# Attention scores in four hand-turned PSUM banks, and weight and operand work spread over the head pairs of a fused attention and two-layer feed-forward kernel

## The chip, the cores and the metric

One core of a Trainium2 chip runs the whole program in one launch. The metric is the device time of one execution in microseconds; the median over the runs is compared. Engines: TensorE (PE, its weight loads PEld), VectorE (DVE), ScalarE (ACT), GpSimd (POOL), and SyncE (SP), whose queue issues nearly all DMAs.

## The reference

```python
batch, n_heads, seq, head_dim = (4, 8, 576, 64)
def _attn_ref(q, k, v, f):
    scores = scale * np.matmul(q, k.transpose(0, 1, 3, 2))
    cum = np.cumsum(np.log(np.clip(f, 0.0001, 1.0)), axis=-1)
    decay = cum[:, :, :, None] - cum[:, :, None, :]
    scores = np.where(causal, -1000000000.0, scores + decay)
    scores = scores - np.max(scores, axis=-1, keepdims=True)
    attn = np.exp(scores)
    attn = attn / (np.sum(attn, axis=-1, keepdims=True) + 1e-09)
    return np.matmul(attn, v)
# x = attention as 2304 rows of 512, then two layers, d_ff = 2048:
# h = x @ w_in;  g = h * clip(h + 3, 0, 6) / 6;                    x = g @ w_out
# h = x @ w_in2; g = max(h, 0) + alpha * min(h, 0);              out = g @ w_out2
```

## The kernel before

There are 16 head pairs (4 batches of 4 pairs, two heads of 64 columns each). The attention runs over 144 units, nine to a pair: positions 0 to 3 are four blocks of 128 query rows of the even head, position 4 is the tail (the last 64 query rows of both heads together, against all 576 keys, in two halves of 288 columns), positions 5 to 8 are the odd head's four blocks. A loop over steps `t` runs a software pipeline in a fixed order on every engine: at step `t` PE transposes the probabilities of unit `t-5`, DVE takes the negated row maximum of unit `t-1` (`maxes`), ACT takes the exponentials with row sums of unit `t-2` (`exps`), ACT or DVE copies the transposed probabilities out of PSUM (`evac`), then the work due at this step (`todo`) and the score matmuls of unit `t` (`stage1`) are issued, and last what a table puts beside the step (`aside`). Nothing is reordered later: each engine works its list from the front.

The scores of a unit go to one of four PSUM banks in turn (`ps_sc`); the tail takes two. A bank is written again four or three units later, once the exponential that reads it is done.

Due work by its position in a pair: at 3 and 7, POOL scales and copies the next head's q and k (`prep_head`, tiles q1, k1); two steps later POOL forms the low part of k (`low_k`); `low_q`, on DVE, forms the low part of q (tile q2) for the even head at position 6 and the odd head at position 0. `recips` (position 2, of the pair before) inverts the row sums on DVE and widens them on POOL (tile rw), `spread` (5) transposes rw on PE and copies it to rcb, `stage3` (6 and 8) multiplies the transposed probabilities with v into one PSUM bank (pv), and DVE writes pv times rcb into r, the layer input.

Beside the units runs preparation for the first layer. A weight step converts 128x512 packed 64-bit weights to f32: m on ACT, then f, s, j, g on DVE; sums S1 to S4 on POOL, casts h on ACT, low parts l on POOL. `build_parts` makes seven sums of blocks of r: a (in place, POOL), h (cast, ACT), l (low part, POOL), each for two columns. The tables `CONV_ATT` and `CONV_ATT1` and the list `places` give the step of each; a name such as `j1 34` is step j of weight chunk 1 at step 34.

After the attention, PE works without a break through the two layers (lines 633 on), 24 sets of products and pieces in each; the last attention steps (`DRAIN`) already issue the first products.

Of the kernel before, what the change touches and what calls it, by code (L numbers as in the profile page):

```python
# [8 lines left out]
F32 = mybir.dt.float32  # L9
# [4 lines left out]
AF = mybir.ActivationFunctionType  # L14
# [7 lines left out]
def decay_attention_ffn2_kernel(ctx, tc, qk, v, f, wi1, wo1, wi2, wo2, alpha, out):  # L22
# [22 lines left out]
    DRAIN = {9 * NP + 3: 2, 9 * NP + 4: 2, 9 * NP + 6: 2, 9 * NP + 7: 2}  # L45
    CONV_ATT = "m0 22 f0 23 s0 24 j0 25 g0 26 m1 31 f1 32 s1 33 j1 34 g1 35 hb 37 lb 39 S1 42 S3 42 S2 45 S4 45 ha 51 la 54 hc 53 lc 60 hd 60 ld 63 m2 69 f2 70 s2 71 j2 72 g2 73 m3 78 f3 79 s3 80 j3 81 g3 83 ho0 78 lo0 87 ho1 87 lo1 91 wi0 90 wi1 93 wo0 99 wo1 102 r0 54 r1 63 r2 93 r3 104"
    CONV_ATT1 = "r0 131 r1 141 m0 108 f0 109 s0 110 j0 114 g0 115 m1 117 f1 118 s1 119 j1 123 g1 124 S1 143 S3 145 S2 146 ha 146 hc 146 hb 147 la 147 lc 147 lb 148 S4 149 hd 149 ld 150 m2 150 f2 151 s2 151 j2 152 g2 153 m3 151 f3 152 s3 153"
    CONV_FIRST = "j3 0 g3 1 ho0 2 lo0 4 ho1 5 lo1 7 wi0 30 wi1 33 wo0 36 wo1 38"
    CONV_A = "m0 0 f0 2 s0 3 j0 4 g0 5 m1 4 f1 6 s1 7 j1 8 g1 9"
# [69 lines left out]

    def conv_ops(ff, g, cache=False, held=()):  # L120

        ops, stage = {}, {}

        def f32(s):

            if s not in stage:
                tag = {0: "wa", 1: "wb", 2: "wc", 3: "wb", "S": "wc"}[s]
                if cache:
                    tag = ("wa", "wb", "wc")[(4 * g + s) % 3]
                stage[s] = wtmp.tile([128, KH, 256], F32, tag=tag, name=tag)  # L130
            return stage[s]
# [146 lines left out]
    def attention():  # L278
        with ExitStack() as ax:
            rx = ExitStack()  # L280
            rawp = rx.enter_context(tc.tile_pool(name="rawp", bufs=3, side="right"))
            opsp = rx.enter_context(tc.tile_pool(name="opsp", bufs=3, side="right"))
            ps_sc = rx.enter_context(tc.tile_pool(name="ps_sc", bufs=4, space=PSUM, side="right"))
            vp = ax.enter_context(tc.tile_pool(name="vp", bufs=2))
# [54 lines left out]

            def maxes(parts, dsts):  # L340
                n = len(parts)
                nm = st.tile([128, 2], F32, tag="nm", name="nm")
# [4 lines left out]
                return parts, dsts, nm  # L347

            def exps(parts, dsts, nm):
                pt = pp.tile([128, S], F32, tag="p", name="p")  # L350
                for i, (src, c0, cw) in enumerate(parts):
                    nc.scalar.activation(out=pt[:, c0:c0 + cw], in_=src, func=AF.Exp, bias=nm[:, 0:1],  # L352
                                         scale=1.0, accum_out=dsts[i])
                return (pt,)

            def stage1(u):
                p, ab, i = u
                if p not in sm:
                    sm[p] = sums.tile([128, 10], F32, tag="sm", name="sm")
                ss = sm[p]  # L360
                if ab < 2:
                    q1, q2, k1, k2 = slots[2 * p + ab]
                    w = 128 * (i + 1)
                    n = max(w, 256)
                    sc = ps_sc.tile([128, 512], F32, tag="sc", name="sc")
                    qs = slice(128 * i, 128 * i + 128)
                    nc.tensor.matmul(out=sc[:, 0:n], lhsT=q1[:, qs], rhs=k1[:, 0:n], start=True, stop=False)  # L367
                    nc.tensor.matmul(out=sc[:, 0:n], lhsT=q2[:, qs], rhs=k2[:, 0:n], start=False, stop=False)  # L368
                    nc.tensor.matmul(out=sc[:, w - 128:w], lhsT=identb, rhs=maskb, start=False, stop=True)  # L369
                    c = 5 * ab + i  # L370
                    return [(sc[:, 0:w], 0, w)], [ss[:, c:c + 1]]
                parts = []
                hw = S // 2
                for c in range(2):
                    sc = ps_sc.tile([128, 512], F32, tag="sc", name="sc")
                    ks = slice(hw * c, hw * c + hw)
                    for a in range(2):
                        q1, q2, k1, k2 = slots[2 * p + a]
                        nc.tensor.matmul(out=sc[:, 0:hw], lhsT=q1[:, 512:640], rhs=k1[:, ks],
                                         start=(a == 0), stop=False)  # L380
                        nc.tensor.matmul(out=sc[:, 0:hw], lhsT=q2[:, 512:640], rhs=k2[:, ks],
                                         start=False, stop=(a == 1 and c == 0))
                    if c == 1:
                        nc.tensor.matmul(out=sc[:, hw - TAIL:hw], lhsT=identb, rhs=maskj, start=False, stop=True)
                    parts.append((sc[:, 0:hw], hw * c, hw))
                return parts, [ss[:, 4:5], ss[:, 9:10]]

# [31 lines left out]
            def recips(p):  # L419

                ss = sm.pop(p)
                rc = st.tile([128, 10], F32, tag="rc", name="rc")
# [5 lines left out]
                rw = rcp.tile([128, KT, 2, 64], F32, tag="rw", name="rw")  # L428
                scaled(
                    "P", rw, rc.rearrange("p (a i) -> p i a", a=2).unsqueeze(3).broadcast_to([128, KT, 2, 64]))  # L430
                rcs[p] = rw

            def spread(p):

                rw = rcs.pop(p)
# [132 lines left out]
            aside(18, lambda: fetch(1))  # L568
            ops = conv_ops(0, 0, held=(0, 1, 2, 3))
            for name, t in table(CONV_ATT):  # L570
                aside(t, ops[name])
            early["first"] = conv_ops(0, 1, held=(0, 1))
# [4 lines left out]
            for k, (a, h) in enumerate(zip(("", "l0", "l1", "l2", "a3", "a4", "a6", "l3", "l4", "a5", "l6", "l5"),  # L577
                                           ("0", "1", "2", "", "", "", "3", "4", "6", "", "5", ""))):
                for c in range(KH):
                    if a:  # L580
                        aside(places[k], {"l": lows, "a": adds}[a[0]][int(a[1]), c])
                    if h:
                        aside(places[k], highs[int(h), c])
            for t in range(len(units) + max(LV, PB) + 1):
# [13 lines left out]
                if t < len(units):  # L598
# [333 lines left out]
```

## Time and profile before

| | us |
|---|---|
| median of 3 runs | 977.1 (976.98 to 977.2) |
| the profiled execution | 978.46 |
| its span, first to last instruction | 975.4 |
| PE, DVE, ACT, POOL busy in the span | 959.3, 698.8, 539.3, 594.4 |
| granted TensorE clock | 1.0 throughout |

So 3.06 us of the profiled execution lie outside its span, and it took 1.36 us more than the median. A busy matmul is a pipelined one whose end is modelled: rows of PE overlap, and its share of busy time says little. A stretch from one pair's tail to the next pair's tail, cut at the start of the tail's masking matmul (L384), is the unit in which the attention is read below; there are 15 such stretches, and the first has no `stage3` in it.

### The profile page before, as it was taken

To read this page: it belongs to the slowest core of one execution; us is meant where nothing else is said; L and a number is where in the kernel's file an instruction comes from. 1 tells how busy PE (TensorE), PEld (TensorE's weight loads), DVE (VectorE), ACT (ScalarE), POOL (GpSimd) and SP (SyncE) were. 2 spreads that over 40 slices of the span, in tenths; PEclk is the share of its full clock that TensorE was granted. 3 is DMA by queue.
4 is the path that set the end of the run, shared out by engine and by line. 5 is a ranking of instruction groups with operands and counts; after the bars stand their busy time and mean duration, and the time that the engine had idled before them with its cause. 6 is when DMAs were issued, how large, how long until landed. Compare 5 with 4: busy or idle time off the path is not lost.

```text
span 975.4 us, 15895 instructions
## 1 busy us (share of the span) xinstructions
PE 959.3 (98%) x5524; PEld 858.9 (88%) x5525; DVE 698.8 (72%) x1275; ACT 539.3 (55%) x1348; POOL 594.4 (61%) x583
## 2 busy tenths in 40 slices
PE   8999999999999999999999999999999999999998
PEld 5767666678999999999999999989899989989897
DVE  7998878857688777876788665357898778635454
ACT  5778787866555554555564356644455546343231
POOL 7577589957655666487576289556646658422231
PEclk9999999999999999999999999999999999999999
DMA  6656586401424444210578722413524410253541
GB/s 214 217 146 213 158 273 203 151 1 44 162 90 182 184 166 161 107 66 1 173 281 301 289 91 107 162 65 143 196 95 182 184 66 23 97 205 141 215 162 65
DMA packets 36195, 145.79 MB, mean 149 GB/s; under 512 B 4860, under 2 KB 4860, under 8 KB 33012
## 3 DMA queue, kind: packets, MB, share of 16 engines
q1 hardware_dynamic: 36112, 144.79, 42.2%
q8 instruction: 43, 0.70, 0.3%
q14 instruction: 36, 0.29, 0.1%
q10 hardware_dynamic: 4, 0.00, 0.0%
HBM read 97.21 MB, written 43.42 MB: 144 GB/s over the span
## 4 chain that ended last, share of the span: by engine, by line
PE 85%; DVE 7%; POOL 3%; ACT 2%; issue 2%; DMA 1%; SPq 0%; POOLq 0%; DVEq 0%; ACTq 0%
PE o L762 21%; PE hA L722 20%; PE o L760 19%; PE hC L722 10%; PE hB L722 5%; PE pv L457 4%; PE tp L400 2%; DVE nm L344 2%; PE sc L367 2%; PE sc L368 1%; DVE q L336 1%; ACT p L352 1%; POOL xl L248 1%; DVE r L240 1%; DVE pt L411 0%
## 5 line engine op out<-in xcount | busy, mean ns | idle before, releaser
L705 POOL TENSOR_TENSOR g<-t,g 128x384 fp32r<-128x384 f32 x192 | 205.3, 1070 | 285.6 <-ACT g L704 269.1
L760 PE MATMUL o<-g,wo 128*128 128x384 f32 x1152 | 231.0, 339 | 2.1 <-POOL g L705 1.2
L722 PE MATMUL hA<-xh,wi 128*128 128x384 f32 x768 | 224.3, 338 | 0.7 <-ACT s L727 0.4
L762 PE MATMUL o<-wo,g 128*128 128x512 f32 x864 | 223.2, 394 | 0.0
L760 PEld LDWEIGHTS o<-g,wo 128*128 128x128 f32 x1152 | 203.9, 188 | 3.6 <-POOL g L705 1.8
L704 ACT CAST g<-t 128x384 fp32r<-128x384 f32 x192 | 98.7, 514 | 177.5 <-DVE t L699 92.6
L762 PEld LDWEIGHTS o<-wo,g 128*128 128x128 f32 x864 | 160.6, 188 | 25.7
L780 DVE TENSOR_TENSOR r<-o,r 128x512 f32<-128x512 f32 x126 | 86.6, 688 | 86.3 <-PE o L762 85.9
L722 PEld LDWEIGHTS hA<-xh,wi 128*128 128x128 f32 x768 | 141.5, 188 | 4.4 <-ACT s L727 0.7
L722 PE MATMUL hA<-xl,wi 128*128 128x384 f32 x384 | 129.6, 337 | 0.0
L769 DVE SCALAR_TENSOR_TENSOR r<-o,r 128x384 f32<-128x384 f32 x168 | 91.9, 552 | 45.8 <-PE o L760 45.0
L722 PE MATMUL hC<-xh,wi 128*128 128x384 f32 x384 | 114.1, 338 | 0.0
L352 ACT ACTIVATE p<-sc,nm 128x128 f32<-128x128 f32 (+4 forms) x160 | 84.1, 529 | 20.7 <-DVE nm L344 17.3
L344 DVE TENSOR_REDUCE nm<-sc 128x1 f32<-128x128 f32 (+4 forms) x160 | 71.4, 469 | 6.2 <-PE sc L369 4.0
L722 PEld LDWEIGHTS hA<-xl,wi 128*128 128x128 f32 x384 | 72.1, 188 | 3.2
L722 PEld LDWEIGHTS hC<-xh,wi 128*128 128x128 f32 x384 | 70.9, 188 | 2.1 <-issue 0.2
L248 POOL TENSOR_TENSOR xl<-r,xh 128x384 fp32r<-128x384 f32 x59 | 68.9, 1185 | 2.0 <-ACT xh L243 1.5
L400 PE MATMUL tp<-ident,p 128*128 128x128 f32 x384 | 67.6, 279 | 1.1 <-ACT pt L416 0.6
L727 ACT COPY s<-hA 128x384 f32<-128x384 f32 x96 | 45.8, 477 | 34.7 <-PE hA L722 34.4
L722 PE MATMUL hC<-xl,wi 128*128 128x384 f32 x192 | 64.8, 337 | 0.0
L367 PE MATMUL sc<-k,q 128*128 128x256 f32 (+2 forms) x128 | 53.7, 420 | 4.7 <-ACT p L352 3.6
L722 PE MATMUL hB<-xh,wi 128*128 128x384 f32 x192 | 57.1, 338 | 0.0
(136 smaller groups left out, 1724.6 us busy)
## 6 DMA issues: line engine op xcount, KB each, us to landing
wid<-wi SPq DMA_DIRECT2D x24, 896.0 KB
wi<-wid SPq DMA_DIRECT2D x12, 1792.0 KB
rqk<-in_qk SPq DMA_DIRECT2D x32, 608.0 KB
raw<-in_wi SPq DMA_DIRECT2D x32, 512.0 KB
raw<-in_wo SPq DMA_DIRECT2D x32, 512.0 KB
wod<-wo SPq DMA_DIRECT2D x24, 512.0 KB
wo<-wod SPq DMA_DIRECT2D x12, 1024.0 KB
vt<-in_v SPq DMA_DIRECT2D x16, 320.0 KB
```

The source lines that it names most:

```text
L248: e.tensor_sub(out=XS[k][1][:, b, c], in0=x, in1=XS[k][0][:, b, c].bitcast(F32))
L344: nc.vector.tensor_reduce(out=nm[:, i:i + 1], in_=src, axis=AX.X, op=ALU.max, negate=True)
L352: nc.scalar.activation(out=pt[:, c0:c0 + cw], in_=src, func=AF.Exp, bias=nm[:, 0:1], scale=1.0, accum_out=dsts[i])
L367: nc.tensor.matmul(out=sc[:, 0:n], lhsT=q1[:, qs], rhs=k1[:, 0:n], start=True, stop=False)
L400: nc.tensor.transpose(tp[:, j, :], pt[:, 128 * j:128 * j + 128], ident)
L704: nc.scalar.copy(out=gt[n][i][:, 0], in_=hold["g"])
L705: nc.gpsimd.tensor_sub(out=gt[n][i][:, 1], in0=hold["g"], in1=gt[n][i][:, 0].bitcast(F32))
L722: nc.tensor.matmul(out=h, lhsT=a, rhs=b[:, x, kc], start=new and kc + e == 0, stop=kc == KH - 1 and e == 2, skip_group_check=not new)
L760: nc.tensor.matmul(out=o[:, 0:NB], lhsT=a[:, cs], rhs=b, start=st, stop=sp)
L762: nc.tensor.matmul(out=o, lhsT=b[:, cs], rhs=a, start=st, stop=sp)
L769: later(0, lambda: nc.vector.scalar_tensor_tensor(out=acc, in0=o[:, 0:NB], scalar=1.0 / 6.0, in1=acc, op0=ALU.mult, op1=ALU.add))
L780: nc.vector.tensor_add(out=acc, in0=o, in1=acc)
```

## The change

The four score banks become one tile with waits written by hand (the same waits between PE, DVE and ACT as before). The tail's two halves lie in neighbouring banks and are read by one maximum and one exponential over 576 columns, so the minimum of two maxima, the addition of two row sums and a copy go; the row sums need 9 columns in place of 10, rw 512 in place of 640, and the tail's reciprocal goes to PE straight from rc. `low_q` of the even head is issued in front of `stage3` at its step. The tables are new: f and s of a weight chunk now share one step, j and g one step a pair later; the casts h stand about a pair ahead of, or behind, what they go with; the seven sums are spread from the third pair on; one more weight chunk (m2 of `CONV_ATT1`) is moved into the attention. The staging tiles of a weight set get a fourth buffer, wd.

```diff
-    CONV_FIRST = "j3 0 g3 1 ho0 2 lo0 4 ho1 5 lo1 7 wi0 30 wi1 33 wo0 36 wo1 38"
+    BUILD_ATT = "h00 26 l00 32 h01 35 l01 41 h10 44 l10 50 h11 53 l11 79 a30 79 h20 80 a31 88 h21 89 l20 95 a40 97 l21 97 h30 98 l30 104 a41 106 h31 107 h40 107 l31 113 l40 115 a60 115 h41 116 l41 122 a61 124 a50 124 h60 125 a51 130 l60 131 h61 134 h50 134 h51 134 l61 139 l50 140 l51 142"
+    CONV_FIRST = "ho0 0 lo0 2 ho1 4 lo1 6 wi0 30 wi1 33 wo0 36 wo1 38"
...
-                tag = {0: "wa", 1: "wb", 2: "wc", 3: "wb", "S": "wc"}[s]
+                tag = "w" + tags[(0, 1, 2, 3, "S").index(s)]
...
-            ps_sc = rx.enter_context(tc.tile_pool(name="ps_sc", bufs=4, space=PSUM, side="right"))
+            ps_sc = rx.enter_context(tc.tile_pool(name="ps_sc", bufs=1, space=PSUM, side="right"))
+            banks = ps_sc.tile([128, 4, 512], F32, name="sc")
...
-                for i, (src, c0, cw) in enumerate(parts):
-                    nc.vector.tensor_reduce(out=nm[:, i:i + 1], in_=src, axis=AX.X, op=ALU.max, negate=True)
-                if n == 2:
-                    nc.vector.tensor_scalar(out=nm[:, 0:1], in0=nm[:, 0:1], scalar1=nm[:, 1:2], scalar2=None, op0=ALU.min)
+                src = banks[:, b, 0:w] if n == 1 else banks[:, b:b + n, 0:w]
+                last = waits("V", nc.vector.tensor_reduce(out=nm, in_=src, axis=AX.X if n == 1 else AX.XY, op=ALU.max,
+                                                     negate=True), last)
...
-                for i, (src, c0, cw) in enumerate(parts):
-                    nc.scalar.activation(out=pt[:, c0:c0 + cw], in_=src, func=AF.Exp, bias=nm[:, 0:1],
-                                         scale=1.0, accum_out=dsts[i])
+                o = pt[:, 0:src.shape[-1]] if n == 1 else pt.rearrange("p (n w) -> p n w", n=n)
+                last = waits("A", nc.scalar.activation(out=o, in_=src, func=AF.Exp, bias=nm, scale=1.0, accum_out=dst), last)
+                for x in range(b, b + n):
+                    reader[x] = last
...
-                nc.vector.tensor_scalar(out=ss[:, 4:5], in0=ss[:, 4:5], scalar1=ss[:, 9:10], scalar2=None,
-                                        op0=ALU.add)
-                nc.vector.tensor_copy(out=ss[:, 9:10], in_=ss[:, 4:5])
...
-                nc.tensor.transpose(tj[:, 0, :], rw[:, 4].rearrange("p a b -> p (a b)"), ident)
+                nc.tensor.transpose(tj[:, 0, :], rc[:, 8:9].broadcast_to([128, 128]), ident)
...
-            places = [9 * p + o for p in range(9, NP) for o in (5, 9)][1:]
...
+            for name, t in table(BUILD_ATT):
+                aside(t, {"h": highs, "l": lows, "a": adds}[name[0]][int(name[1]), int(name[2])])
...
-                        todo.setdefault(t + QL + 1, []).append(lambda h=2 * p + 2: low_q(h))
+                        todo.setdefault(t + QL + 1, []).insert(0, lambda h=2 * p + 2: low_q(h))
```

DVE from the 13th to the 14th reciprocal, before: nm is the negated maximum, q the low part of q, pt the transposed probabilities, wb a weight chunk.

```order
L427 RECIPROCAL rc<-rc 128x10
L145 TENSOR_SCALAR wb<-wb 128x512
L344 TENSOR_REDUCE nm<-sc 128x1 x2
L411 COPY pt<-tp 128x4x128
L344 TENSOR_REDUCE nm<-sc 128x1 x2
L346 TENSOR_SCALAR nm<-nm 128x1
L344 TENSOR_REDUCE nm<-sc 128x1
L464 TENSOR_TENSOR r_82<-pv,rcb 128x256
L336 SCALAR_TENSOR_TENSOR q_2921<-rqk,q_2920 64x640
L149 SCALAR_TENSOR_TENSOR wb<-raw,wb 128x512
L344 TENSOR_REDUCE nm<-sc 128x1
L154 SCALAR_TENSOR_TENSOR wb<-raw,wb 128x512
```

The same stretch of DVE now; the rest of the pair follows in the order of before, less the addition and the copy of row sums.

```order
L443 RECIPROCAL rc<-rc 128x9
L364 TENSOR_REDUCE nm<-sc 128x1 x2
L430 COPY pt<-tp 128x4x128
L364 TENSOR_REDUCE nm<-sc 128x1 x2
L357 SCALAR_TENSOR_TENSOR q_2729<-rqk,q_2728 64x640
L480 TENSOR_TENSOR r_82<-pv,rcb 128x256
L364 TENSOR_REDUCE nm<-sc 128x1
L150 SCALAR_TENSOR_TENSOR wc<-raw,wc 128x512
L155 SCALAR_TENSOR_TENSOR wc<-raw,wc 128x512
```

One maximum and the minimum are gone, q stands in front of r, and j and g of a chunk stand together with no s before them.

POOL over the pair before that, from one rw to the next: xl and r_80 are low parts and sums of the layer input, k the copies and low parts of k. Before:

```order
L93 TENSOR_SCALAR rw<-rc 128x640
L93 TENSOR_SCALAR q_2711<-rqk 128x640
L93 TENSOR_SCALAR k_2713<-rqk 128x576
L331 TENSOR_TENSOR k_2713<-rqk,k_2713 64x576
L240 TENSOR_TENSOR r_80<-r_80 128x384 x2
L93 TENSOR_SCALAR q_2805<-rqk 128x640
L93 TENSOR_SCALAR k_2807<-rqk 128x576
L331 TENSOR_TENSOR k_2807<-rqk,k_2807 64x576
L240 TENSOR_TENSOR r_80<-r_80 128x384 x2
```

And now:

```order
L94 TENSOR_SCALAR rw<-rc 128x512
L94 TENSOR_SCALAR q_2539<-rqk 128x640
L94 TENSOR_SCALAR k_2541<-rqk 128x576
L352 TENSOR_TENSOR k_2541<-rqk,k_2541 64x576
L249 TENSOR_TENSOR xl_79<-r_80,xh_78 128x384
L94 TENSOR_SCALAR q_2624<-rqk 128x640
L94 TENSOR_SCALAR k_2626<-rqk 128x576
L249 TENSOR_TENSOR xl_79<-r_80,xh_78 128x384
L241 TENSOR_TENSOR r_80<-r_80 128x384
L352 TENSOR_TENSOR k_2626<-rqk,k_2626 64x576
```

Four block instructions beside the pair's own have become three.

## Rows read from the trace of the kernel before

**Rows 1.** Stretches from tail to tail: busy time by engine, clock, DMA share, GB/s.

```profile
core 0: us, PE busy (x) PEld busy (x) DVE busy (x) ACT busy (x) POOL busy (x), PEclk, DMA share, GB/s
24.10:84.95 60.85, 59.55 (x458) 42.47 (x456) 54.34 (x118) 47.06 (x173) 41.28 (x44) 1.00 0.61 190
84.95:195.95 111.00, 106.56 (x822) 76.15 (x820) 92.89 (x213) 87.63 (x319) 90.83 (x87) 1.00 0.63 195
84.95:96.39 11.44, 11.44 (x94) 8.41 (x92) 9.13 (x24) 9.01 (x35) 8.77 (x10) 1.00 0.71 215
...
157.39:170.65 13.26, 11.95 (x93) 8.44 (x92) 12.36 (x27) 9.95 (x37) 12.47 (x12) 1.00 0.50 144
...
195.95:225.00 29.05, 27.09 (x185) 21.93 (x183) 15.74 (x34) 18.95 (x54) 14.91 (x17) 1.00 0.09 34
```

**Rows 2.** Who waited for whom, 24 to 196: us in total, times, longest.

```profile
ACT p L352 <- DVE nm L344: 16.1, 24, 2.0
...
DVE r L464 <- PE pv L457: 9.2, 10, 1.7
...
DVE r L464 <- ACT p L352: 7.6, 10, 0.9
PEld sc L367 <- ACT p L352: 6.2, 10, 1.2
...
PEld tj L442 <- DVE pt L411: 2.5, 6, 0.7
```

**Rows 3.** DVE groups by shape, 24 to 196: busy us, mean ns, idle before.

```profile
L344 DVE TENSOR_REDUCE nm<-sc 128x1 f32<-128x512 f32 x29 | 19.8, 683 | 1.4 <-PE sc L369 1.4
...
L344 DVE TENSOR_REDUCE nm<-sc 128x1 f32<-128x288 f32 x28 | 11.4, 446 | 0.0
...
L346 DVE TENSOR_SCALAR nm<-nm 128x1 f32<-128x1 f32 x14 | 3.0, 214 | 0.5
...
L423 DVE TENSOR_SCALAR sm<-sm 128x1 f32<-128x1 f32 x14 | 2.7, 195 | 0.0
...
L425 DVE COPY sm<-sm 128x1 f32<-128x1 f32 x14 | 2.1, 154 | 0.5
```

**Rows 4.** ACT groups by shape, 0 to 225.

```profile
L352 ACT ACTIVATION_READ_ACCUMULATOR p<-sc,nm 128x1 f32 x160 | 32.7, 204 | 0.0
L352 ACT ACTIVATE p<-sc,nm 128x512 f32<-128x512 f32 x32 | 22.2, 693 | 1.6 <-DVE nm L344 1.6
...
L352 ACT ACTIVATE p<-sc,nm 128x288 f32<-128x288 f32 x32 | 15.7, 497 | 0.4
```

**Rows 5.** POOL by line, 24 to 196: duration ns min/median/max, first and last start.

```profile
L93 POOL TENSOR_SCALAR q<-rqk x28: 719/724/1293, 24.7 to 188.9; 128x640 fp32r<-128x640 f32 x28
L93 POOL TENSOR_SCALAR k<-rqk x28: 666/672/1267, 25.4 to 189.6; 128x576 fp32r<-128x576 f32 x28
L93 POOL TENSOR_SCALAR rw<-rc x15: 724/725/944, 24.0 to 194.7; 128x640 f32<-128x640 f32 x15
...
L331 POOL TENSOR_TENSOR k<-rqk,k x28: 1398/1407/1461, 26.1 to 190.3; 64x576 fp32r<-64x576 f32 x28
...
L240 POOL TENSOR_TENSOR r<-r x8: 1005/1380/2122, 153.0 to 187.3; 128x384 f32<-128x384 f32 x8
```

**Rows 6.** DVE by line, 24 to 196, likewise.

```profile
L336 DVE SCALAR_TENSOR_TENSOR q<-rqk,q x28: 804/928/1598, 27.6 to 191.5; 64x640 fp32r<-64x640 f32 x28
...
L141 DVE TENSOR_SCALAR wa<-wa x2: 406/954/1503, 37.3 to 154.8; 128x512 f32<-128x512 f32 x2
...
L149 DVE SCALAR_TENSOR_TENSOR wc<-raw,wc x1: 676/676/676, 104.8 to 104.8; 128x512 uint32<-128x512 uint32 x1
```

**Rows 7.** Timelines of DVE and of POOL, 122.9 to 126: start us, us.

```profile
123.45 1.57 DVE L336 SCALAR_TENSOR_TENSOR q<-rqk,q 64x640 fp32r<-64x640 f32 x1
...
123.06 1.28 POOL L187 TENSOR_TENSOR wo<-wc,wo 128x512 fp32r<-128x512 f32 x1
124.32 1.29 POOL L93 TENSOR_SCALAR q<-rqk 128x640 fp32r<-128x640 f32 x1
```

**Rows 8.** What POOL waited for, 120 to 196.

```profile
POOL rw L93 <- DVE rc L427: 3.6, 3, 2.2
```

More of the change, by code (lines that the diff above doesn't have):

```diff
@@ L118, in fetch, with conv_ops @@
             nc.sync.dma_start(out=raws[wseq[k]], in_=wsrc[ff][s // 2][g][:, 512 * (s % 2):512 * (s % 2) + 512])
-    def conv_ops(ff, g, cache=False, held=()):
+    def conv_ops(ff, g, cache=False, held=(), tags="abdbc"):
         ops, stage = {}, {}
@@ L282, in attention, with waits, score_banks @@
             opsp = rx.enter_context(tc.tile_pool(name="opsp", bufs=3, side="right"))
-            ps_sc = rx.enter_context(tc.tile_pool(name="ps_sc", bufs=4, space=PSUM, side="right"))
+            ps_sc = rx.enter_context(tc.tile_pool(name="ps_sc", bufs=1, space=PSUM, side="right"))
+            banks = ps_sc.tile([128, 4, 512], F32, name="sc")
+            turn, reader = [0], {}
+            def waits(engine, ins, *deps):
+                ins = getattr(ins, "ins", ins)
+                for d in deps:
+                    tc.add_manual_dep(ins, d.name, mybir.DependencyInfo(mybir.DependencyClass.Sync, mybir.DependencyReason.DATA))
+                for e in "TVA".replace(engine, ""):
+                    tc.declare_no_dep(ins, group="scores" + e, keep=list(deps), reason="other banks")
+                tc.add_to_no_dep_group("scores" + engine, ins)
+                return ins
+            def score_banks(n):
+                b = [(turn[0] + i) % 4 for i in range(n)]
+                turn[0] += n
+                assert b[-1] == b[0] + n - 1
+                return b[0], [reader[x] for x in range(b[0], b[0] + n) if x in reader]
             vp = ax.enter_context(tc.tile_pool(name="vp", bufs=2))
@@ L338, in low_q, with maxes, exps @@
                     op0=ALU.mult, op1=ALU.subtract)
[L340 to L349 removed]
+            def maxes(b, n, w, dst, last):
+                nm = st.tile([128, 1], F32, tag="nm", name="nm")
+                src = banks[:, b, 0:w] if n == 1 else banks[:, b:b + n, 0:w]
+                last = waits("V", nc.vector.tensor_reduce(out=nm, in_=src, axis=AX.X if n == 1 else AX.XY, op=ALU.max,
+                                                     negate=True), last)
+                return b, n, src, dst, nm, last
+            def exps(b, n, src, dst, nm, last):
                 pt = pp.tile([128, S], F32, tag="p", name="p")
[L351 to L353 removed]
+                o = pt[:, 0:src.shape[-1]] if n == 1 else pt.rearrange("p (n w) -> p n w", n=n)
+                last = waits("A", nc.scalar.activation(out=o, in_=src, func=AF.Exp, bias=nm, scale=1.0, accum_out=dst), last)
+                for x in range(b, b + n):
+                    reader[x] = last
                 return (pt,)
@@ L358, in stage1 @@
                 if p not in sm:
-                    sm[p] = sums.tile([128, 10], F32, tag="sm", name="sm")
+                    sm[p] = sums.tile([128, 9], F32, tag="sm", name="sm")
                 ss = sm[p]
@@ L364, in stage1 @@
                     n = max(w, 256)
-                    sc = ps_sc.tile([128, 512], F32, tag="sc", name="sc")
+                    b, free = score_banks(1)
+                    sc = banks[:, b]
                     qs = slice(128 * i, 128 * i + 128)
[L367 to L372, printed above, removed]
+                    waits("T", nc.tensor.matmul(out=sc[:, 0:n], lhsT=q1[:, qs], rhs=k1[:, 0:n], start=True, stop=False), *free)
+                    waits("T", nc.tensor.matmul(out=sc[:, 0:n], lhsT=q2[:, qs], rhs=k2[:, 0:n], start=False, stop=False))
+                    last = waits("T", nc.tensor.matmul(out=sc[:, w - 128:w], lhsT=identb, rhs=maskb, start=False, stop=True))
+                    c = 4 * ab + i
+                    return b, 1, w, ss[:, c:c + 1], last
                 hw = S // 2
+                b, free = score_banks(2)
                 for c in range(2):
-                    sc = ps_sc.tile([128, 512], F32, tag="sc", name="sc")
+                    sc = banks[:, b + c]
                     ks = slice(hw * c, hw * c + hw)
@@ L378, in stage1 @@
                         q1, q2, k1, k2 = slots[2 * p + a]
[L379 to L386, printed above, removed]
+                        waits("T", nc.tensor.matmul(out=sc[:, 0:hw], lhsT=q1[:, 512:640], rhs=k1[:, ks],
+                                               start=(a == 0), stop=False), *(free[c:c + 1] if a == 0 else ()))
+                        waits("T", nc.tensor.matmul(out=sc[:, 0:hw], lhsT=q2[:, 512:640], rhs=k2[:, ks],
+                                               start=False, stop=(a == 1 and c == 0)))
+                last = waits("T", nc.tensor.matmul(out=sc[:, hw - TAIL:hw], lhsT=identb, rhs=maskj, start=False, stop=True))
+                return b, 2, hw, ss[:, 8:9], last
             def pt_tile(h):
@@ L421, in recips @@
                 ss = sm.pop(p)
-                rc = st.tile([128, 10], F32, tag="rc", name="rc")
-                nc.vector.tensor_scalar(out=ss[:, 4:5], in0=ss[:, 4:5], scalar1=ss[:, 9:10], scalar2=None,
-                                        op0=ALU.add)
-                nc.vector.tensor_copy(out=ss[:, 9:10], in_=ss[:, 4:5])
+                rc = st.tile([128, 9], F32, tag="rc", name="rc")
                 nc.vector.tensor_scalar(out=rc, in0=ss, scalar1=1e-9, scalar2=None, op0=ALU.add)
                 nc.vector.reciprocal(out=rc, in_=rc)
[L428 to L431, printed above, removed]
+                rw = rcp.tile([128, 4, 2, 64], F32, tag="rw", name="rw")
+                scaled("P", rw, rc[:, 0:8].rearrange("p (a i) -> p i a", a=2).unsqueeze(3)
+                       .broadcast_to([128, 4, 2, 64]))
+                rcs[p] = rw, rc
             def spread(p):
-                rw = rcs.pop(p)
+                rw, rc = rcs.pop(p)
                 t = rcp.tile([128, S], F32, tag="rcb", name="rcb")
@@ L568, in attention @@
             aside(18, lambda: fetch(1))
-            ops = conv_ops(0, 0, held=(0, 1, 2, 3))
+            ops = conv_ops(0, 0, held=(0, 1, 2, 3), tags="abdac")
             for name, t in table(CONV_ATT):
                 aside(t, ops[name])
-            early["first"] = conv_ops(0, 1, held=(0, 1))
+            early["first"] = conv_ops(0, 1, held=(0, 1), tags="bcdba")
             for name, t in table(CONV_ATT1):
@@ L575, in attention @@
             adds, highs, lows = build_parts(0, 0, nc.gpsimd, (nc.gpsimd,))
-            places = [9 * p + o for p in range(9, NP) for o in (5, 9)][1:]
[L577 to L583, printed above, removed]
+            for name, t in table(BUILD_ATT):
+                aside(t, {"h": highs, "l": lows, "a": adds}[name[0]][int(name[1]), int(name[2])])
             for t in range(len(units) + max(LV, PB) + 1):
```

4 lines of the change are left out of this document (2 added, 2 removed).

## The prediction

> **What bounds the kernel now.** I read the share of the span by engine first, then the attention pair by pair (busy time in stretches), then who waited for whom, then single durations, and last two engines side by side in time. The feed-forward part is left alone: the diff moves nothing there but a buffer's name, and PE runs through it. What can move is the attention.
>
> Fourteen stretches from tail to tail, 24.10 to 195.95, carry the same work on PE and take 60.85 + 111.00 = 171.85 us, 12.28 each [rows 1]. The quickest, 84.95 to 96.39, takes 11.44, and in it PE has no idle time at all; I take 11.44 as what PE alone needs for a pair. At that pace fourteen pairs take 160.2, so 11.7 us of the attention are waiting. The reader is to see who is late in a slow pair: from 157.39 to 170.65 DVE is busy 12.36 and POOL 12.47 of 13.26 us, while in the quick one they are busy 9.13 and 8.77 [rows 1]. The way from there to PE [rows 2]: ACT's exponential waits for DVE's maximum (16.1 us), and PE's next score, held at its weight load, for the exponential that still reads its bank (6.2 us, 10 times, longest 1.2); a second way is the bank of the reciprocal's transpose, which waits for DVE's copy (2.5 us). These two make 8.7 of the 11.7.
>
> DVE and POOL are not late independently. A q of DVE that begins beside a POOL subtraction takes 1.57 us, and the POOL scaling that begins under it 1.29 [rows 7]; the same two take 0.80 and 0.72 at their shortest [rows 5, 6]. Each stands while the other works. So for the DVE instructions that show this (q, and f and j of a weight step, whose shortest and longest or neighbouring durations differ as widely), the two engines are one resource, and what counts in a pair is POOL's time plus DVE's time in them, at their shortest durations.
>
> **The joint load, before.** POOL's own work per pair is two of each head operation, 2 x (0.72 + 0.67 + 1.41) = 5.6, and rw 0.73, so 6.3 [rows 5]. In the late pairs four block sums or low parts come to it at 1.0 each: 10.3. DVE adds two q at 0.80, 1.6, and, where a whole weight chunk falls into the pair, f and s at about 0.4 and j and g at about 0.68 (s and g taken like their neighbours) [rows 6], 2.2. That makes 14.1 in the pair that took 13.26: the load explains the length, to within 0.8 that does overlap. A late pair without weight work has 11.9.
>
> **The change part by part.**
>
> *Tail read at once.* DVE loses two maxima of 446 ns, the minimum of 214, an addition of 195 and a copy of 154, and gets one maximum over 576 columns [rows 3]. No row shows that one: between 288 and 512 columns a column costs (683 - 446) / 224 = 1.06 ns, so 576 cost 751; bounds are 683 (not less than 512 columns) and 892 (two halves, nothing saved). I take 751, since the line is straight there. DVE saves 892 + 214 + 349 - 751 = 0.70 us a pair. ACT loses two exponentials of 497 and two accumulator reads of 204 for one of each over 576 [rows 4]: by the same line 749 + 204, a saving of 0.45; bounds 693 and 994 for the exponential. POOL's rw shrinks by a fifth, 0.15. None of this lies on PE, so it is worth something only where DVE is late. The banks of the tail come free together: the first one after 751 + 749 = 1.50 where it now takes 446 + 446 + 214 + 497 = 1.60. The first half never was early, because its exponential waits for both maxima.
>
> The Trainium skill (Perfetto Trace Analysis, "Optimizing Scalar/DVE Operations") says that larger operations pay where the engine is saturated, and that breaking them up can let work finish sooner where it only causes bubbles elsewhere. Rows 1 show both kinds of pair. By its second half the merge would cost the five early pairs up to half an exponential, 0.25 us each or 1.2 in all; by the 1.50 against 1.60 it costs nothing, which I hold to.
>
> *The transpose of the tail's reciprocal* reads one column repeated. No row shows such a weight load. From below it saves the wait for rw, already inside the 11.7; from above, if it took twice as long as the transpose beside it, some 0.15 a pair, 2 us in all. I take nothing.
>
> *q in front of r.* DVE stands idle in front of r for 9.2 us waiting for pv and for 7.6 waiting behind ACT [rows 2], with q queued behind. Now q fills that time. What is late next is r, by at most one q, 0.8 to 1.6 us [rows 6]; pv is not written again until two steps on, about 2.5 us (11.44 over nine steps, twice). If that cover went, PE would wait at pv once a pair. What q itself waits for, POOL's q1, is three steps older. I give it no term of its own: it makes DVE's lateness smaller in the term below.
>
> *The tables.* POOL in a late pair now has 6.2 and at most three extra instructions, 9.2 (two pairs 9.5). DVE has q and half a weight chunk, f and s or j and g: 0.8 or 1.4. The joint load is 11.6 or 12.2, 11.9 on average over the late pairs, 12.4 at most, against 14.1 before. The early pairs, 24.10 to 84.95, get builds they did not have: POOL 7.2 to 8.4, joint 9 to 11. DVE's total there falls by 0.70 for the tail and gains half a chunk in every pair instead of a whole one in some. ACT's casts and m keep their number, now grouped behind the exponential of position 6, while PE is in the long second part of `stage3`. On SP's queue raw fetches and weight stores change places with q2 and k2 loads; PE waits for no DMA in these stretches, so nothing.
>
> *Sum.* The late nine pairs, 111.00 us or 12.33 each, come near the floor, but the load of 11.9 leaves no slack: in the pair above the length was 0.94 of the load, which would be 11.2, under the floor. I take 11.95, half a microsecond above it: 9 x 0.38 = 3.4 us. The early five, 12.17 each, with less DVE work than PE time: 11.7, so 5 x 0.47 = 2.4 us. Bounds for any pair: the floor from below; from above its length today, or the load with nothing overlapping and POOL's wait for the reciprocal on top. The 29.05 us from 195.95 to 225 [rows 1] have the same PE order and DVE busy only 15.74; one weight chunk less there is covered: nothing, plus or minus 1. In all 5.8 us: span 975.4 - 5.8 = 969.6, execution 978.46 - 5.8 = 972.7. The profiled execution lies 1.36 above the median of the runs, so the median becomes 977.1 - 5.8 = 971.3 us.
>
> **The rivals.**
>
> *All waiting goes.* Every pair runs at 11.5. For it: the load times 0.94 is under the floor everywhere. Against it: even today's light pairs average 12.17. 171.85 - 161.0 = 10.9 us, a time of 966.2.
>
> *The lumps eat the gain.* Two weight instructions now stand together on DVE, and each can stand for POOL: f up to 1.50, s by its side nearly as long again [rows 6]. The maximum behind them is late by 2.4 us instead of 1.5. For it: ACT's longest wait for a maximum today is 2.0 and PE's longest behind it 1.2 [rows 2]. Against it: the lump stands at position 7, while PE does the second part of `stage3`, and the unit behind it has four units before its bank is wanted. If each of the fourteen pairs keeps 0.8 above the floor, it is 12.25 again: 976.5 to 977.
>
> *Slower: the joint load plus POOL's wait.* POOL works its list from the front, and rw waits there for DVE's reciprocal: 1.2 us a time where it happens in the late stretch [rows 8]. While POOL stands, DVE is not helped, if nothing of the joint work is left to do there. Were that idle time paid in each of the nine late pairs on top of a load of 11.9 that overlaps nowhere, they would take 13.1, 0.77 more than today, 6.9 in all; with 2.4 won early it is 4.5 slower, 981.6. It decides from a wait of 0.7 us a pair. Against it: where POOL is loaded its queue is late and the reciprocal is there first; rows 8 have three such waits in six pairs.
> The Trainium skill (SBUF — State Buffer, "Who interferes with whom") states that exclusion: a port pair shared by VectorE and GpSimd is held for a whole instruction, and whoever comes second stands until the end. The trace agrees, 0.80 against 1.57 us; by that rule nothing of the joint load overlaps, and this rival gets its chance from it.
>
> **How the numbers follow.** The forecast, some of the waiting gone, a gain of 3 to 9 us: 0.59, its own range 968 to 974. All of it gone: 0.17. No change: 0.14. Slower: 0.10. About 0.2%, 2 us, is what a measurement of this kernel tells from no change, so faster is 0.59 + 0.17 = 0.76, same 0.14, slower 0.10. The range leaves out the lower half of the full gain and the slower case with a little of no change: 966.5 to 977.3.
>
> **What would show it.** Right: the stretches from tail to tail in the late half take 11.6 to 12.2 each and none 13; POOL's busy time there falls under 11; waits of PE's score loads for the exponential fall from 6.2 us to under 3; a 576-column maximum of about 0.75 us and an exponential of about 0.75; r no longer waits long for pv. Wrong: stretches of 12.3 and more with f, s or j, g and q of DVE stretched beside POOL; PE waiting at pv for r; POOL idle a microsecond a pair in front of rw; or a stretch from 196 to the first layer that grows by what the attention won.

## The result, and the profile after

| | before | after |
|---|---|---|
| median of 4 runs each, one chip, us | 977.15 (976.98 to 977.22) | 965.16 (964.37 to 965.78) |
| span of the profiled execution, us | 975.4 | 963.4 |

The ratio is 0.9872 (95% interval 0.9861 to 0.9884): 12 us faster. The forecast was 971.3, with a range down to 966.5, so the time lies below the range; the gain is twice the 5.8 us that were forecast.

The span gives back 12.0 us: 0.2 before the first cut, 10.2 in the fourteen stretches (171.85 to 161.62 us), and 1.5 behind the last tail. First the stretches, with the columns of [rows 1]: all early five, their first one, all late nine, the longest of these and two usual ones.

```profile
23.88:81.77 57.89, 57.72 (x458) 42.11 (x456) 49.81 (x96) 46.55 (x165) 39.07 (x41) 1.00 0.68 211
23.88:35.93 12.05, 11.88 (x94) 8.44 (x92) 9.95 (x19) 9.92 (x35) 7.56 (x10) 1.00 0.90 298
...
81.77:185.50 103.73, 103.71 (x822) 75.88 (x820) 97.80 (x178) 85.74 (x298) 93.03 (x90) 1.00 0.67 205
93.19:104.66 11.47, 11.47 (x93) 8.42 (x92) 10.82 (x20) 9.56 (x34) 10.77 (x10) 1.00 0.50 141
127.59:139.52 11.93, 11.91 (x93) 8.47 (x92) 11.35 (x21) 9.78 (x33) 9.97 (x11) 1.00 0.78 253
...
162.57:174.04 11.47, 11.47 (x93) 8.42 (x92) 10.94 (x20) 9.57 (x34) 10.76 (x11) 1.00 0.59 177
```

In the late half PE is now busy 103.71 of 103.73 us, where it was busy 106.56 of 111.00. The usual pair takes 11.47, PE's own time, although DVE and POOL are each busy 10.8 us in it. So the two may be nearly full; what counts is that neither has more than a pair holds. POOL stays under 11 us in all nine late pairs. The longest of them is the one in which DVE has 11.35.

Who waited for whom in the stretches, 24 to 186; to be read against [rows 2, 8].

```profile
ACT p L371 <- DVE nm L364: 9.8, 18, 1.5
...
POOL rw L94 <- DVE rc L443: 5.3, 6, 1.7
DVE r L480 <- PE pv L473: 4.1, 7, 1.5
...
PEld sc L400 <- ACT p L371: 0.4, 2, 0.3
PEld tj L458 <- DVE pt L430: 0.4, 1, 0.4
```

PE's wait at a score bank went from 6.2 us to 0.4, now at the tail's banks (L400), and that for the copy of pt from 2.5 to 0.4. DVE stands in front of r for 4.1 us instead of 9.2 + 7.6. The exponential still waits 9.8 us for the maximum, but no longer so late that PE notices.

The tail's single reads, in the DVE and ACT groups by shape, beside DVE's q and r, 24 to 186:

```profile
L357 DVE SCALAR_TENSOR_TENSOR q<-rqk,q 64x640 fp32r<-64x640 f32 x28 | 31.1, 1111 | 0.2 <-issue 0.2
L364 DVE TENSOR_REDUCE nm<-sc 128x1 f32<-128x576 f32 x15 | 11.3, 756 | 1.8 <-PE sc L404 1.7
```

```profile
L371 ACT ACTIVATE p<-sc,nm 128x576 f32<-128x576 f32 x14 | 10.4, 742 | 0.4
```

Behind the attention the 1.5 us are mostly one wait of PE, 1.3 us, for the copy r that frees its output bank o:

```profile
PEld o L760 <- ACT r L767: 1.3, 1, 1.3
```

Here are DVE and ACT in the kernel before, 218 to 225 (start, duration, in brackets the idle time before and what ended it); t and g are steps of the first layer's activation function.

```profile
218.23 0.68 DVE L149 SCALAR_TENSOR_TENSOR wc<-raw,wc 128x512 uint32<-128x512 uint32 x1
...
221.05 0.69 DVE L149 SCALAR_TENSOR_TENSOR wb<-raw,wb 128x512 uint32<-128x512 uint32 x1
221.66 0.55 DVE L696 SCALAR_TENSOR_TENSOR t<-t,hA 128x384 f32<-128x384 f32 x1
...
222.24 0.52 ACT L704 CAST g<-t 128x384 fp32r<-128x384 f32 x1 [2.93 <-DVE t L696]
...
223.85 0.62 ACT L183 CAST wo<-wc 128x512 fp32r<-128x512 f32 x1
224.37 0.87 ACT L767 ACTIVATE r<-o 128x384 f32<-128x384 f32 x2
```

And the same place after, where PE's wait for r is not there any more:

```profile
207.52 0.68 DVE L150 SCALAR_TENSOR_TENSOR wb<-raw,wb 128x512 uint32<-128x512 uint32 x1
208.23 1.40 DVE L155 SCALAR_TENSOR_TENSOR wb<-raw,wb 128x512 uint32<-128x512 uint32 x1
209.55 0.54 DVE L706 SCALAR_TENSOR_TENSOR t<-t,hA 128x384 f32<-128x384 f32 x1
...
208.13 0.61 ACT L184 CAST wo<-wd 128x512 fp32r<-128x512 f32 x1
...
210.13 0.51 ACT L714 CAST g<-t 128x384 fp32r<-128x384 f32 x1 [1.01 <-DVE t L706]
...
211.75 0.87 ACT L777 ACTIVATE r<-o 128x384 f32<-128x384 f32 x2
```

Before, five steps of two weight chunks (j, f, g, s, j) stood on DVE in front of t. ACT waited 2.93 us for t with r behind it in its list, and a weight cast then stood in front of r. Now two steps stand in front of t, ACT waits 1.01 us, and the cast is over 3 us before r begins. The cast held r up by 0.5 us (223.85 to 224.37), less than PE's wait of 1.3, so most of the wait came through DVE and t. This is read from the two traces; no run parts the cast from DVE's steps. CONV_FIRST and the chunk moved into the attention took both from there.

### The profile page after: what moved, and what is told of

It reads as the page before. It is cut to its first block, busy times and chain, and to the rows that moved or that the text cites. A ratio compares the mean times of both kernels' runs of the same rounds, so it can differ in the third digit from the quotient of the medians.

```text
span 963.4 us, 15758 instructions
## 1 busy us (share of the span) xinstructions
PE 953.9 (99%) x5525; PEld 858.4 (89%) x5525; DVE 698.6 (73%) x1211; ACT 536.3 (56%) x1316; POOL 595.3 (62%) x583
## 4 chain that ended last, share of the span: by engine, by line
PE 93%; POOL 2%; DVE 2%; DMA 1%; issue 1%; ACT 1%; SPq 0%; POOLq 0%; DVEq 0%; ACTq 0%
PE o L772 21%; PE hA L732 20%; PE o L770 19%; PE hC L732 10%; PE hB L732 5%; PE pv L473 5%; PE tp L419 5%; PE sc L388 3%; PE sc L389 2%; PE sc L390 1%; PE sc L400 1%; PE sc L402 1%; PE tr L455 1%; POOL xl L249 1%; DVE r L241 0%
## 5 line engine op out<-in xcount | busy, mean ns | idle before, releaser
L371 ACT ACTIVATE p<-sc,nm 128x128 f32<-128x128 f32 (+2 forms) x144 | 80.3, 560 | 16.0 <-DVE nm L364 12.1
L364 DVE TENSOR_REDUCE nm<-sc 128x1 f32<-128x128 f32 (+2 forms) x144 | 71.1, 507 | 11.7 <-PE sc L390 7.5
L746 DVE TENSOR_TENSOR hC<-hC,s 128x384 f32<-128x384 f32 x48 | 27.1, 564 | 40.7 <-PE hC L732 38.8
```

Source lines behind the costliest of these rows:

```text
L364: last = waits("V", nc.vector.tensor_reduce(out=nm, in_=src, axis=AX.X if n == 1 else AX.XY, op=ALU.max, negate=True), last)
L371: last = waits("A", nc.scalar.activation(out=o, in_=src, func=AF.Exp, bias=nm, scale=1.0, accum_out=dst), last)
```

## Experiments

Each was timed in rounds against the kernel before, on the same chip (977.46 to 977.64 us there); four chips were used in all. "Early", "late" and "rest" are cut as above, at each trace's tails: the first five stretches, the next nine, and what lies behind them. The first cut lies anywhere from 23.8 to 25.9 us. This is no effect of the edits alone: d3 differs from after only from the third pair on, and its first cut is at 25.6 where that of after is at 23.9. Small prices are therefore read from the late column. These three columns come from one execution of each kernel.

| run | median us | ratio (95%) | early | late | rest |
|---|---|---|---|---|---|
| before | 977.15 | | 60.85 | 111.00 | 779.5 |
| after | 965.16 | 0.9872 (0.9861 to 0.9884) | 57.89 | 103.73 | 777.9 |
| e1 merge alone | 975.32 | 0.9976 (0.9966 to 0.9985) | 59.86 | 110.40 | 779.2 |
| e2 q first alone | 978.03 | 1.0005 (0.9996 to 1.0013) | 60.95 | 111.73 | 779.4 |
| e3 tables alone | 972.04 | 0.9943 (0.9931 to 0.9956) | 57.31 | 109.95 | 777.9 |
| e4 halves apart | 966.37 | 0.9884 (0.9871 to 0.9898) | 58.25 | 104.00 | 777.9 |
| e5 q behind r | 970.53 | 0.9931 (0.9918 to 0.9943) | 58.02 | 108.12 | 777.8 |
| e6 old tables | 974.40 | 0.9970 (0.9958 to 0.9982) | 59.07 | 110.25 | 779.3 |
| e7 old weight tables | 970.73 | 0.9932 (0.9920 to 0.9945) | 58.95 | 105.77 | 779.3 |
| e8 old places of sums | 970.33 | 0.9930 (0.9918 to 0.9942) | 57.83 | 108.86 | 777.7 |
| d1 second maximum | 967.37 | 0.9898 (0.9883 to 0.9913) | 57.81 | 105.25 | 777.9 |
| d2 second even q | 979.43 | 1.0019 (1.0010 to 1.0028) | 61.98 | 113.92 | 777.7 |
| d3 second k on POOL | 968.75 | 0.9908 (0.9895 to 0.9922) | 57.31 | 107.54 | 777.7 |
| d4 second odd q | 977.58 | 0.9999 (0.9990 to 1.0008) | 58.81 | 114.37 | 778.8 |
| d5 spare maximum, even | 970.31 | 0.9924 (0.9911 to 0.9936) | 58.06 | 107.91 | 777.9 |
| d6 spare maximum, odd | 968.87 | 0.9909 (0.9895 to 0.9922) | 58.12 | 107.78 | 777.9 |

**One part alone, on the kernel before.** e1 is before with the four-bank tile, the tail read at once and what goes with it (the narrower rw, the tail's reciprocal from rc), and nothing else of the change; e2 is before with one line changed:

```diff
-                        todo.setdefault(t + QL + 1, []).append(lambda h=2 * p + 2: low_q(h))
+                        todo.setdefault(t + QL + 1, []).insert(0, lambda h=2 * p + 2: low_q(h))
```

> Before with the hand-turned banks alone (tail read at once, narrower rw): tables and q as before. If q in front of r carries the 3 us of the run with old tables: 976.5 to 977.5 us. If the tail does: 974 to 975.

> Before with the even head's q in front of r alone. If the value of q's place (5.4 us beside the new tables) is its own: 971 to 973 us. If it needs level pairs, since in the overloaded late ones DVE's time goes to standing for POOL whatever stands in front: 975 to 977 us.

The merge alone is worth 2.3 us, q alone nothing that the runs can tell. Neither touches the slowest pairs: the longest is 13.34 in e1 and 13.56 in e2, for 13.26 before.

**One part undone, in the kernel after.** e3 has the tables alone (halves apart, q behind r; the tile of four banks, the 512 columns of rw and the way of the tail's reciprocal stay as changed, and no run tries these three by themselves), e4 reads the halves apart, e5 puts q behind r again, e6 has all old tables, e7 the old weight tables, e8 the old places of the sums.

```diff
# e4 (and e3)
+                for i in range(n):
+                    got = waits("V", nc.vector.tensor_reduce(out=nm[:, i:i + 1], in_=banks[:, b + i, 0:w], axis=AX.X,
+                                                             op=ALU.max, negate=True), last)
...
# e5 (and e3)
-                        todo.setdefault(t + QL + 1, []).insert(0, lambda h=2 * p + 2: low_q(h))
+                        todo.setdefault(t + QL + 1, []).append(lambda h=2 * p + 2: low_q(h))
# e7 (and e6): CONV_ATT, CONV_ATT1, CONV_FIRST and the tags as before
# e8 (and e6)
-            for name, t in table(BUILD_ATT):
+            places = [9 * p + o for p in range(9, NP) for o in (5, 9)][1:]
...
```

> The new tables and tags alone: the tail's halves are read apart and q stands behind r, as before (only rw is narrower and the tail's reciprocal goes to PE without it). Theory J: most of the 12 us is here, 966 to 969 us. Rival D: DVE is as loaded as before in the mean, so 972 to 976 us.

> The change with the tail's two halves read apart again (two maxima, a minimum, two exponentials, one addition of row sums a pair); tables, q in front of r and the narrower rw stay. Theory J: the maxima read PSUM and don't stand for POOL, so the level tables still hide nearly all: 965.2 to 967 us. Rival D: 0.55 us more of DVE in each of 16 pairs shows: 968 to 971 us.

> The change with the even head's q behind r again, all else as changed. Theory J: DVE waits about 0.8 us a pair in front of r, with slack of about 2 us behind it: 965 to 967 us. Rival D: DVE loses 0.8 us a pair in every pair: 968 to 972 us.

> The change with the four tables and the staging tags of before: the tail read at once and q in front of r stay. Theory J (what made pairs slow was POOL's time plus DVE's time in the instructions that stand for POOL, and the tables levelled it): the late pairs keep a joint load of up to 14, they stay at 12.5 to 13, and the time is 972 to 975. Rival D (DVE alone was late, and the 0.7 us a pair saved on the tail plus the filled wait in front of r cured it): 966 to 969 us.

> The change with the weight tables and staging tags of before (whole weight chunks fall into single pairs again), but the new spread of the layer-input sums. Theory J (level joint load of DVE and POOL): the pairs with a whole chunk grow by 0.7 to 1 us, the others stay at 11.5: 968 to 971. Rival S (the spread of the sums on POOL did it, the weight tables nothing): 965 to 966.5 us. If the gain of 1.2 us behind the attention is of the weight tables' casts, that is lost here too.

> The change with the layer-input sums in their old places (four to a late pair), the weight tables new. Theory J: POOL gets 10.3 and its weight work on top in the late pairs, so these take 12.5 to 13.5: 971 to 976 us. Rival C (the weight tables did it): 965 to 967 us.

Three things follow. First, the tables are the largest part: alone they give 5.5 of the 12 us (e3), without them 3.1 are left (e6), and both halves are needed, since either old one gives back over 5 us (e7, e8). In e8 the late half and its longest stretch read:

```profile
81.92:190.78 108.86, 105.19 (x821) 76.03 (x820) 95.81 (x178) 87.04 (x304) 97.27 (x94) 1.00 0.65 196
152.75:165.80 13.05, 11.99 (x93) 8.49 (x92) 11.37 (x21) 9.21 (x34) 12.73 (x14) 1.00 0.82 240
```

POOL has 14 instructions and 12.73 us there, more than PE's 11.5; eight of e8's other stretches stay at 11.5 or less. So it is not the sum over the half that decides, but what falls into one pair. e7 gives back 1.4 us of the rest too: ACT waits 2.93 us for t again, the cast stands in front of r, and PE's wait for r, 1.3 us, is back.

Second, q in front of r is worth 5.4 us by the medians (970.53 against 965.16), 4.4 of them in the late half, once the tables are level; before that it is worth nothing (e2), or 0.9 beside the merge (e6 against e1, with intervals that overlap). The waits of e5, 24 to 196, and its late half:

```profile
ACT p L371 <- DVE nm L364: 23.3, 33, 1.5
DVE r L480 <- PE pv L473: 13.6, 15, 1.5
...
PEld sc L400 <- ACT p L371: 3.0, 11, 0.6
...
DVE r L480 <- ACT p L371: 1.3, 1, 1.3
```

```profile
83.94:192.06 108.12, 106.87 (x822) 76.70 (x820) 96.16 (x179) 85.55 (x300) 91.70 (x90) 1.00 0.65 195
```

DVE stands 13.6 + 1.3 us in front of r with q behind it, its maxima come late, and PE is held at the tail's bank. Why e2 gains nothing, though q is out of r's way there too, is not shown. Its trace says that DVE still stands 15.2 us in front of r, that the 28 q take 34.2 us where they took 30.5 before, and that DVE and POOL are busy 13.18 and 12.77 us of its longest pair, of 13.56. So q may have traded one wait for another there.

Third, the merge is worth 1.2 us at the end of the list (after against e4), 1.5 beside the tables (e5 against e3), both with intervals that overlap, and 2.3 alone. It takes work from DVE; that this is worth the less, the less DVE is late, fits these three, but is not shown by them.

**One cost doubled, in the kernel after**, from the third pair on (d1 in every pair), to see how near each engine is to its limit. d1 takes the tail's maximum twice, and the exponential waits for the second; d2 the even head's q (in front of r), d4 the odd head's q, d3 POOL's scaling of the even head's k; d5 and d6 put an unused maximum over rqk behind the q that d2 and d4 double.

```diff
# d2, even; d4 the same with h % 2 == 1
+                for again in range(2 if h >= 4 and h % 2 == 0 else 1):
+                    nc.vector.scalar_tensor_tensor(
+                        out=q2[0:64], in0=rq[0:64], scalar=SCALE, in1=q1[0:64].bitcast(F32),
+                        op0=ALU.mult, op1=ALU.subtract)
# d5, even; d6 the same with h % 2 == 1
+                if h >= 4 and h % 2 == 0:
+                    spare = st.tile([128, 1], F32, tag="spare", name="spare")
+                    nc.vector.tensor_reduce(out=spare[0:64], in_=rq[0:64], axis=AX.X, op=ALU.max, negate=True)
# d3
+                for again in range(2 if h >= 4 and h % 2 == 0 else 1):
+                    scaled(e[1], k1, rk)
```

> The change with the tail's maximum taken twice, into a scratch column: 0.75 us more of DVE a pair, read from PSUM, 12 us in all. Theory L (a pair stays at 11.47 until DVE's or POOL's list of the pair, with the time it stands for the other, passes about 11.3): DVE is busy 10.8 to 11.3 in the late nine, so these grow by 0.2 to 0.5 each and the five early ones not at all: 967 to 970 us. Rival P (PE alone sets the pair, DVE has slack): 965.2 us; rival D (each DVE microsecond counts): 977 us.

> The change with the even head's low part of q taken twice from the third pair on: 14 more DVE instructions with two operands in SBUF, 0.80 us each at their shortest, nearly as much as the extra maximum. Theory L with joint load: it also stands for POOL and makes POOL stand, 0.8 to 1.5 us a pair on both lists: the late pairs grow by 0.6 to 1.0: 970 to 975 us, clearly more than the extra maximum. If only DVE's own time counted it would cost what the extra maximum costs, within 1 us.

> The change with the even head's POOL scaling of k done twice from the third pair on: 14 POOL instructions of 0.67 us at their shortest. Theory J (POOL's time and DVE's time in what stands for POOL add up): the late nine pairs go from a load of 11.9 to 12.6 and grow by 0.2 to 0.6 each: 967 to 971 us. Rival L (each engine's own list counts): POOL was busy 10.8 of 11.47, so 11.5 now, and the pairs grow by 0.1 or not at all: 965 to 966.5 us.

> The change with the odd head's low part of q taken twice (two SBUF operands, it stands for POOL, 0.80 us at its shortest), at position 0, where no r is behind it. If the 14 us of the doubled even q were the joint load, this one costs about the same, 975 to 980 us. If they were its place in front of r and the pv bank, this one costs what DVE's lateness costs, 2 to 6 us: 967 to 971.

> The change with one spare maximum of 64x640 from SBUF (one operand, about 0.75 us) behind the even head's q, so in front of r. Place theory: r is late by 0.75 us and PE waits at the pv bank: 970 to 977 us. Joint-load theory: one operand doesn't stand for POOL, so 967 to 969 us as the extra maximum of the tail.

> The change with the same spare maximum behind the odd head's q, at position 0. Both theories: like the extra maximum of the tail, 966.5 to 968.5 us; against the doubled odd q it tells what standing for POOL adds at one place: by theory J 2 us or more, by rival L under 1.

A second q costs 14.3 us (d2) or 12.4 (d4), more than the whole change gave, a spare maximum at the same places 5.2 (d5) or 3.7 (d6). Both last 0.80 us at their shortest. By line in d4 (q), then in d6 (spare), 24 to 196, ns as min/median/max:

```profile
L358 DVE SCALAR_TENSOR_TENSOR q<-rqk,q x42: 806/988/2072, 26.0 to 194.1; 64x640 fp32r<-64x640 f32 x42
```

```profile
L362 DVE TENSOR_REDUCE spare<-rqk x14: 801/803/805, 32.8 to 186.8; 64x1 f32<-64x640 f32 x14
```

The maximum never stretches, q does up to 2.07 us. The late halves of d4 and d6:

```profile
82.75:197.12 114.37, 108.19 (x821) 76.98 (x820) 107.66 (x188) 85.15 (x300) 92.16 (x91) 1.00 0.62 187
```

```profile
81.97:189.75 107.78, 106.36 (x821) 76.79 (x820) 101.01 (x188) 85.07 (x300) 92.40 (x91) 1.00 0.66 200
```

With the same number of instructions on each engine and POOL equally busy, DVE is busy 6.65 us longer in d4, and the half is 6.6 us longer. Most of it, 5.4 us, lies in q and the spare maximum. By shape, in these halves, d4 and then d6:

```profile
L358 DVE SCALAR_TENSOR_TENSOR q<-rqk,q 64x640 fp32r<-64x640 f32 x27 | 35.4, 1309 | 0.3
```

```profile
L357 DVE SCALAR_TENSOR_TENSOR q<-rqk,q 64x640 fp32r<-64x640 f32 x18 | 22.7, 1264 | 0.0
...
L362 DVE TENSOR_REDUCE spare<-rqk 64x1 f32<-64x640 f32 x9 | 7.2, 802 | 0.0
```

Nine more q lengthen DVE's work by 1.4 us each, nine maxima by 0.80: the difference is time in which DVE stands, and it is counted as busy time. Two operands and a written result against one operand and a column is what the two instructions differ in; which of these makes DVE stand was not taken apart. POOL's wait for the reciprocal, the mechanism of the slower rival, does not set the time. In the late halves of before, d4, d6 and d2:

```profile
POOL rw L93 <- DVE rc L427: 11.6, 5, 5.6
```

```profile
POOL rw L94 <- DVE rc L444: 17.2, 8, 2.6
```

```profile
POOL rw L94 <- DVE rc L446: 12.3, 9, 2.5
```

```profile
POOL rw L94 <- DVE rc L444: 5.6, 4, 1.7
```

The halves of d4 and d2 are nearly alike with 17.2 and 5.6 us of this wait, and that of d6, with 12.3, is 6 us shorter than both. The place matters less. In the late half d2 and d4 stand at 113.92 and 114.37, d5 and d6 at 107.91 and 107.78. What it decides is where PE waits: in d2 at the pv bank that r still reads, as the prediction named it for lost cover (24 to 196), in d4 at the tail's score bank (late half).

```profile
PE pv L474 <- DVE r L481: 10.9, 13, 1.3
```

```profile
PEld sc L401 <- ACT p L372: 9.5, 17, 1.4
```

d3 adds 0.67 us to POOL in a pair and costs 3.6, d1 adds 0.76 to DVE from PSUM and costs 2.2. Over half of d3's price lies in one pair, in which POOL has 13.13 us:

```profile
141.78:155.40 13.62, 12.16 (x93) 8.49 (x92) 11.63 (x22) 10.11 (x37) 13.13 (x14) 1.00 0.67 199
```

So after has some slack left, and different amounts for different instructions: five of the nine late pairs take d1's 0.76 us without growing, and none takes the second q of d2 or d4 so.

**What came as expected and what did not.** Theory J, a joint load of DVE and POOL, had the time in its range in e4, e6, e7 and d3, and so had theory L in d1 and the joint load in d4. In e3 and e5 it was too low, and the time came out in the range of rival D, by which DVE's own time counts. e8 took less than J's range, d2 more than L's (979.43 against 975 at most). d5 came out in the range of the place theory, at its low end, and d6 0.4 above its range, with a difference to d4 as J had it. e1 fell between its two ranges, and e2 lies above both of its own. So neither theory alone holds: the loads have to be level, and then the order on DVE decides.

## Why the prediction was right and wrong

**Right: what bounds the attention, and the way.** PE needs 11.44 to 11.47 a pair, the rest was waiting for late maxima, and this is what went: the wait at the score bank fell under 3 us as forecast, POOL's busy time under 11 in every late pair, no stretch takes 13. But seven of the late nine stand at 11.5 or less, below the 11.6 to 12.2 that were named as the sign. The single reads of the tail last 756 and 742 ns; 751 and 749 had been taken from the line through the shorter ones. The early five take 57.89, 11.58 each, for a forecast of 11.7. By the Trainium skill (Perfetto Trace Analysis, "Optimizing Scalar/DVE Operations") breaking an instruction up may be the better form where it causes bubbles elsewhere, which the prediction priced at up to 1.2 us for the early pairs. e4 breaks the tail up and its early five take 58.25 for 57.89, so the trace does not show that here. The repeated-column transpose was not tried by itself; PE's wait there fell to 0.4 us.

**Wrong, the step that failed: q in front of r, "I give it no term of its own".** It has one of 4.4 us in the late half, 5.4 by the medians. The prediction saw that DVE stands 9.2 + 7.6 us there with q behind, and then let the gain vanish in a lateness that it took from load alone ("the load of 11.9 leaves no slack"). e5, which is the kernel without this step, came to 970.53 us, 0.8 from the forecast, with a late half of 108.12 / 9 = 12.01 a pair for the 11.95 that were forecast. But e5 and after carry the same instructions, and so the same load, and after takes 103.73 / 9 = 11.53 a pair. So at this load it was the order on DVE that kept e5's pairs above PE's pace, and that the half microsecond taken for the load comes so near to e5 is luck. (The most loaded pair, given as 12.4, is 12.5 by its own terms; nothing hangs on it.) Idle time in the middle of an in-order list can't be used by what stands behind it: with q in that place DVE's wait in front of r fell from 13.6 + 1.3 us to 4.1, and the fourteen stretches together became 4.5 us shorter.

**Wrong, a small term: from 195.95 on "nothing, plus or minus 1".** It was 1.5 us, 1.3 of them PE's wait for r. The prediction counted DVE's work there, 15.74 of 29.05 us, took it for covered, and looked neither at what stands in front of t on DVE nor at any wait of PE behind 196. e6 and e7, with the old weight tables, lose the gain; the kernels with the new ones keep it, but for d4, whose rest is 778.8 and was not taken apart.

**The rivals.** *All waiting goes* is what happened (966.2 for 965.16), and on its argument, that the load overlaps enough to stay under PE's time. That its number is so near is in part luck: it takes 10.9 us from the stretches, where 10.2 went, and nothing from behind them, where 1.5 went. *The lumps eat the gain* failed: j and g stand together, and take 1.24 and 1.38 us in one of the chunks, and only the pair with DVE at 11.35 is longer than 11.6 in the late half. *Slower* failed too: POOL's wait for the reciprocal fell from 11.6 us to 5.3 in the late half ([rows 8] begin at 120 and leave out 8.0 of the 11.6), and not everything on DVE and POOL excludes the other, as a pair of 11.47 us shows in which they are busy 10.82 and 10.77. With one more q a pair (d4) the late pairs come to 12.71, towards the 13.1 that this rival gave them, but not by that wait. The Trainium skill's rule for it (SBUF — State Buffer, "Who interferes with whom"), that one of DVE and POOL stands while the other holds their shared port, agrees with q's 0.80 to 2.07 us against the spare maximum's 0.80; the page names VectorE operations with two SBUF inputs for it, which q is and the spare maximum is not.

**Still open.** That the three parts are worth more together, 12 us, than alone (2.3, nothing, 5.5) is shown; why q needs level tables first is not, and how the 5.4 us of q divide between r's wait and POOL's standing is not.

## What to carry to other kernels

Budget helper engines pair by pair, not over a stage: PE ran at its own pace with DVE and POOL each busy 94% of a pair, and lost 1.6 us in a pair where POOL had 12.73. Where an engine works in order, look for the wait in the middle of its list and put ready work in front of it; price it only after the loads are level, since before that it may measure as nothing. Work that nobody needs soon should not stand in front of what another engine waits for. An instruction's shortest duration does not tell what one more of it costs where two engines stand for each other.

## What the runs showed of the hardware

One DVE instruction reads 576 columns over two neighbouring PSUM banks in 756 ns, on the line through 288 columns (446) and 512 (683); ACT does so in 742. Of two DVE instructions of 0.80 us on the same 64x640 tile, at the same place, the one with two operands and a full result cost 12.4 us for 14 of them (d4), the one-operand maximum 3.7 (d6).
